# Attention ahead of a mixture of experts: rows of maxima made behind their diagonals, and a pair's first weighted values made in the next pair

## The chip, the cores and the metric

The kernel runs on one core of one Trainium2 chip. The metric is the device time in microseconds: the median of three runs was 2087.34 us (2084.76 to 2088.24). The core's engines are TensorE (PE, its weight loads PEld), VectorE (DVE), ScalarE (ACT), GpSimd (POOL) and SyncE (SP, which here starts transfers).

## The reference

Three stages follow one another. The inputs are q, k, v of shape (4, 8, 576, 64), that is 4 batches of 8 heads; the experts' weights w1 (8, 512, 1024) and w2 (8, 1024, 512); and the weights of a gated unit.

```
attn = softmax(mask(q @ k.T / sqrt(64)))          # mask by blocks of 64: block_i >= block_j
x    = attn @ v                                   # to (2304, 512)
P    = exp(x @ w_gate - max);  8 times: divide by row sums, by column sums, times N / E
out  = sum over e of P[:, e] * (relu(x @ w1[e]) @ w2[e])
y    = (silu(out @ w_gate2) * (out @ w_val2)) @ w_out2
```

The change touches the attention, and the preparation of the first two half-experts' weights that runs beside it.

## The kernel before, in words

The attention works on two heads at once, a pair; there are 16 pairs p, 4 for each batch. Scores are masked in blocks of 64 rows, so a pair has 9 block rows c of growing length. They are worked off in 8 ticks u (TICKS): u = 0 holds block rows 0 and 1, u = 1 holds 2 and 3, u = 2 to 5 hold one each (320 to 512 columns), and u = 6 and 7 hold the two halves of block row 8, 288 columns each. A tick has three thirds (three `yield`s in `attention`):

- first third: the events listed for this tick (`at`), then the scores s_u of pair p on PE, and at u = 6 the first group of weighted values, x_0 (`values(p, 0)`), and its evacuation xf (`take`);
- second third: the transposes t of the tick four earlier, one or two pending items of the split into halves (`work`), the normalising of the tick two earlier (`normalise`, GpSimd's e), the copy a of the transposes by ACT, and the maxima of this tick's scores on DVE (negm, bias);
- last third: at u = 4 the second group x_1 of the pair before and all pending items, and the exponentials e of the tick before on ACT.

Each engine works off its own list in the order in which this generator issues it. Between thirds, `w0.step()` does a step of the weights' preparation of half-experts 0 and 1 (`wowed`, 68 of 129 for each third, 29 steps each half-expert's matrix), and from the first batch's end on `fill` issues the first logits (abc_lg) and matmuls of the first experts on PE (rate 47 of 96).

Scores go to fp16 halves after the fourth pair (from there `st` tiles hold scaled halves; pairs 0 to 3 use fp32 q and k directly). The scale of a pair comes from a maximum over all partitions, which is made in three parts: `across_begin` writes a diagonal d on DVE (L103), `across_mid` multiplies it with ones on PE into a row (qk_a, v_a or w_a, L110), and `across_end` reduces the row on DVE (qk_r, w_r; L116). The row lies in a bank of the scores' pool.

PSUM's banks: three for scores and rows (`ps_s`), one for transposes (`ps_t`), one (`ps_x`) for s_7, x_0, the last transpose t_r and x_1 in turn, and three for the fill. ACT frees the bank of `ps_x` with xf.

`take` scales x_0 or x_1 into xf and appends items to `pend`: three for the first pair of a half, six for the second, which write the halves of the operands xs for the Strassen sums (hi on GpSimd or ACT, lo on GpSimd or DVE). At a batch's end all of them are worked off and `ready` lets `fill` go on with that batch's logits.

Of the kernel before, what the change touches and what calls it, by code (L numbers as in the profile page):

```python
# [9 lines left out]
F32 = mybir.dt.float32  # L10
# [20 lines left out]
def attention_moe_glu_kernel(  # L31
# [22 lines left out]
    B, NPAIR, P, S = qT.shape  # L54
    D = 64
    DM = v.shape[2]
    E, _, FF = w1.shape
# [292 lines left out]
    def expert_items(u):  # L350
# [8 lines left out]
        for i, W in enumerate((W1, W2)):  # L359
            g = {"b": [[None, None], [None, None]]}  # L360
# [34 lines left out]

            tasks = [(0, lambda k=k, mx=mx: mx(k), 1) for k in range(3)]
            tasks += [(0, lambda mx=mx, begin=begin: (mx(3), begin()), 1)]
            tasks += [(0, None, 1), (lambda force, g=g: across_made(g["r"])(force), end, 1)]
            if i == 1 and u < 2:

                def plain_sp(r, c, g=g, sp=sp):
# [403 lines left out]
    def attention(actx):  # L805
# [230 lines left out]
        def values(p, grp):  # L1036
            g = st[p]
            c0, c1 = (0, 4) if grp == 0 else (4, NC)
            a = g["a0"] if grp == 0 else g["a1"]
            nj = (c1 + 1) // 2  # L1040
            n = (c1 - c0) * CB
            x = ps_x.tile([P, 512], F32, tag="x", name=f"x_{p}_{grp}")[:, :n]
            for j in range(nj):
                f = max(c0, 2 * j)
                for h in range(2):
                    nc.tensor.matmul(
                        x[h * D : (h + 1) * D, (f - c0) * CB : n],
                        vt[p][:, j, h * D : (h + 1) * D],
                        a[:, j, f - c0 : c1 - c0, h * CB : (h + 1) * CB],
                        start=j == 0,  # L1050
                        stop=j == nj - 1,
                    )
            return x
# [62 lines left out]

        events = {}

        def at(tick, f, *a):
            events.setdefault(tick, []).append(lambda: f(*a))  # L1120

        for p in range(1, npairs):
            r = p * NTK
            if p < DIRECT:
                if p > 1:
                    at(r - NTK, load_direct, p)
                at(r - 2, lambda p: vt.update({p: load_v(*where(p), "v", 2)}), p)
                continue
            for i in range(2):
                if p > 1:  # L1130
                    at(r - 14 + 1 * i, load_qk, p, i)
                at(r - 11 + 2 * i, max_qk, p, i)
                at(r - 6 + 2 * i, hi_qk, p, i)
                at(r - 5 + 1 * i, lo_qk, p, i)
            at(r - 8, lambda p: across_mid(st[p]["m"]), p)
            at(r - 7, scale_qk, p)
            at(r - 2, lambda p: vt.update({p: load_v(*where(p), "v", 2)}), p)
        for b in range(B):
            r = (b - 1) * NPAIR * NTK
            for i in range(NPAIR):  # L1140
                if b:
                    at(r + i * NTK, scan_load, b, i)
                at(r + i * NTK + 3 if b else 1 + i, scan_max, b, i)
            r = r + NPAIR * NTK - 2 if b else NPAIR
            at(r, scale_v_begin, b)
            at(r + 1, lambda b: across_mid(vmx[b]), b)
            at(r + 2, scale_v_end, b)

        load_direct(0)
        load_direct(1)  # L1150
# [9 lines left out]
        for tk in range(tot + NTK):  # L1160
            p, u = divmod(tk, NTK)
            calm[0] = 0 < u < 5
            for f in events.pop(tk, ()):
                f()
            if on(tk):
                scores(p, u)
            if u == 6 and p < npairs:
                take(p, 0, values(p, 0))
            yield
            out1 = None  # L1170
            if on(tk - 4):
                out1 = transposes(*divmod(tk - 4, NTK))
            work(2 if len(pend) > 6 else 1)
            if on(tk - 2):
                normalise(*divmod(tk - 2, NTK))
            if out1:
                out1()
            if on(tk):
                maxima(p, u)
            yield  # L1180

            if p and u == 4:
                work(len(pend))
                take(p - 1, 1, values(p - 1, 1))
                st.pop(p - 1)
                vt.pop(p - 1)
                if p % NPAIR == 0:
                    work(len(pend))
                    ready[0] = p // NPAIR * S // 2
            if p and u == 3:  # L1190
                rest(p - 1)()
            if on(tk - 1):
                exps(*divmod(tk - 1, NTK))
            yield


# [64 lines left out]
    with tc.manual_schedule():  # L1261
# [67 lines left out]
        with ExitStack() as actx:  # L1329
            yp = actx.enter_context(tc.tile_pool(name="yp", bufs=1))  # L1330
            for _ in attention(actx):
                wowed += 68
                while wowed >= 3 * 43:
                    w0.step()
                    wowed -= 3 * 43
                if ready[0]:
                    owed += rate
                    while owed >= 3 * NTK * NPAIR:
                        next(fill, None)
                        owed -= 3 * NTK * NPAIR  # L1340
            for _ in fill:
                pass
# [411 lines left out]
```

## Time and profile before

| what | value |
| --- | --- |
| median of three runs | 2087.34 us (2084.76 to 2088.24) |
| profiled execution, span from first to last instruction | 2083.4 us |
| attention within it | 0 to 384 us |
| PE, DVE, ACT, POOL busy | 1949.0, 1620.1, 1379.9, 612.8 us |
| mean granted clock of TensorE | 0.983 |

The profiled execution is one run; no other time of it is given than its span, which lacks what lies ahead of the first and behind the last instruction. A timeline's row has the start, the duration from the first to the last of the grouped instructions, the engine, the line, the operation, its output and inputs, the shapes and the count, and in brackets the idle time before it with what ended that. A window's row has the busy time and the number of instructions of each engine, then the granted clock as a share of full speed.

### The profile page before, as it was taken

What the parts mean: (1) busy time and instruction counts of PE and PEld (TensorE: products, weight loads), DVE (VectorE), ACT (ScalarE), POOL (GpSimd) and SP (SyncE); (2) the same over time, 40 slices, a digit from 0 to 9 for tenths busy, and PEclk for the clock granted to TensorE, in tenths of its full rate; (3) what the DMA queues carried; (4) which work ended last, traced back from release to release, by engine and by line L of the source; (5) the groups of instructions that cost most, each with busy time, mean ns of one, the idle gap of its engine ahead of it and who ended that gap; (6) DMA issues with size and microseconds to landing.
All of it is one profiled execution on the core that took longest, in us unless ns stands there. A gap on an engine that the chain in (4) does not pass through costs nothing.

```text
span 2083.4 us, 47251 instructions
## 1 busy us (share of the span) xinstructions
PE 1949.0 (94%) x18378; PEld 1672.9 (80%) x18378; DVE 1620.1 (78%) x3455; ACT 1379.9 (66%) x2940; POOL 612.8 (29%) x873
## 2 busy tenths in 40 slices
PE   6789899799999999999999999999999988999998
PEld 3457676698888888888888888888888877988887
DVE  7887765668787887978878788888887877666666
ACT  5665766348777777878777777777776566544442
POOL 4534444102333333333332333333332123000000
PEclk9889999999999999999999999999999999999999
DMA  5433331306687866878668786777877100301112
GB/s 155 112 96 105 84 105 49 122 22 122 120 172 155 172 136 125 178 150 171 132 132 179 149 178 134 153 157 144 180 148 168 37 11 1 87 21 37 47 42 52
DMA packets 168721, 236.41 MB, mean 113 GB/s; under 512 B 16432, under 2 KB 85680, under 8 KB 168496
## 3 DMA queue, kind: packets, MB, share of 16 engines
q0 software_dynamic: 66560, 107.37, 30.8%
q1 hardware_dynamic: 101936, 126.01, 19.9%
q8 instruction: 144, 2.36, 0.5%
q14 instruction: 81, 0.66, 0.1%
HBM read 90.98 MB, written 24.38 MB: 55 GB/s over the span
## 4 chain that ended last, share of the span: by engine, by line
PE 55%; DVE 15%; ACT 5%; DMA 3%; issue 3%; SPq 0%; POOL 0%; ACTq 0%; DVEq 0%
PE abc_m_b L537 11%; PE m_o_b L645 11%; PE m_o_ac L645 8%; PE abc_m_c L537 5%; PE abc_m_a L537 3%; PE abc_v_b L537 3%; PE abc_g_b L537 3%; PE m_go_b L645 3%; PE m_go_ac L645 2%; DVE m_t L704 2%; DVE m_h L193 2%; DMA wr<-in_w_dram 2%; PE abc_v_c L537 1%; DVE w L182 1%; PE abc_g_c L537 1%
## 5 line engine op out<-in xcount | busy, mean ns | idle before, releaser
L537 PEld LDWEIGHTS <-w 128*128 128x128 f16 x6720 | 609.8, 98 | 110.9 <-issue 45.7
L645 PEld LDWEIGHTS <-m_h 128*128 128x128 f16 x5292 | 514.0, 98 | 69.0 <-issue 10.5
L537 PE MATMUL abc_m_b<-xs,w 128*128 128x256 f16 (+1 forms) x3840 | 476.6, 264 | 31.9 <-DVE m_t L559 29.4
L1443 POOL DMA_DIRECT2D acc<-ev x351 | 305.4, 895 | 581.3 <-ACT ev L1447 367.4
L645 PE MATMUL m_o_b<-w,m_h 128*128 128x256 f16 x3024 | 403.5, 273 | 7.9 <-ACT ev L1447 7.7
L645 PE MATMUL m_o_ac<-w,m_h 128*128 128x256 f16 x2268 | 309.4, 273 | 0.4 <-ACT ev L1447 0.4
L537 PE MATMUL abc_m_c<-xs,w 128*128 128x256 f16 (+1 forms) x1920 | 230.7, 263 | 2.2 <-DVE m_h L758 1.6
L1447 ACT ACTIVATE ev<-m_o_b,pe 128x256 f32<-128x256 f32 x351 | 161.7, 476 | 64.0 <-PE m_o_b L645 52.8
L1447 ACT ACTIVATE ev<-m_o_ac,pe 128x256 f32<-128x256 f32 (+1 forms) x234 | 135.7, 580 | 47.8 <-PE m_o_ac L645 46.4
L178 ACT ACTIVATE w<-wr,ws 128x512 f16<-128x512 f32 x210 | 150.5, 723 | 12.7 <-DVE ws L163 10.3
L182 DVE SCALAR_TENSOR_TENSOR w<-wr,ws,w 128x512 f16<-128x512 f32 x210 | 155.5, 747 | 1.4 <-ACT w L178 1.4
L1431 POOL DMA_DIRECT2D acc<-ev_s x65 | 73.6, 1132 | 259.1 <-ACT ev_s L1427 259.1
L683 ACT CAST m_h<-m_t 128x512 f16<-128x512 f32 (+1 forms) x210 | 121.8, 580 | 41.2 <-DVE m_t L704 40.3
L676 ACT ACTIVATE m_h<-m_t 128x512 f16<-128x512 f32 (+1 forms) x210 | 121.8, 582 | 35.8 <-DVE m_t L574 24.9
L193 DVE TENSOR_TENSOR m_h<-m_t,m_h 128x512 f16<-128x512 f32 (+1 forms) x210 | 133.1, 635 | 8.7 <-ACT m_h L683 8.4
L680 DVE SCALAR_TENSOR_TENSOR m_h<-m_t,m_h 128x512 f16<-128x512 f32 (+1 forms) x210 | 132.2, 635 | 5.8 <-ACT m_h L676 5.6
L537 PEld LDWEIGHTS <-gg_w 128*128 128x128 f16 x1260 | 113.5, 98 | 22.2 <-issue 10.7
L996 POOL TENSOR_SCALAR e<-e,r 128x64 f32<-128x64 f32 (+2 forms) x144 | 78.1, 548 | 166.8 <-DVE r L991 111.9
L645 PEld LDWEIGHTS <-g_h 128*128 128x128 f16 x1134 | 111.0, 99 | 18.9 <-issue 5.4
L537 PEld LDWEIGHTS <-gv_w 128*128 128x128 f16 x1260 | 113.6, 98 | 13.2 <-issue 1.7
L537 PE MATMUL abc_m_a<-xs,w 128*128 128x256 f16 (+1 forms) x960 | 117.5, 262 | 0.0
L375 DVE TENSOR_REDUCE wmx<-wr 128x1 f32<-128x512 f32 x128 | 85.7, 679 | 15.0 <-DMA wr<-in_w_dram 14.9
(298 smaller groups left out, 3364.0 us busy)
## 6 DMA issues: line engine op xcount, KB each, us to landing
acc<-ev POOLq DMA_DIRECT2D x351, 256.0 KB, 4.3
wr<-in_w_dram SPq DMA_DIRECT2D x128, 256.0 KB, 4.8
acc<-ev_s POOLq DMA_DIRECT2D x52, 256.0 KB, 4.3
st<-hl SPq DMA_DIRECT2D x48, 144.0 KB, 3.6
raw_g<-in_w_gate_dram SPq DMA_DIRECT2D x12, 512.0 KB, 5.5
raw_v<-in_w_val_dram SPq DMA_DIRECT2D x12, 512.0 KB, 4.5
raw_o<-in_w_out_dram SPq DMA_DIRECT2D x12, 512.0 KB, 5.0
scr_g<-gg SPq DMA_DIRECT2D x21, 256.0 KB, 2.9
```

The source lines that it names most:

```text
L178: nc.scalar.activation(hi, src, AF.Copy, scale=s)
L182: nc.vector.scalar_tensor_tensor(lo, src, s, hi, op0=ALU.mult, op1=ALU.subtract)
L193: nc.vector.tensor_sub(lo, src, hi)
L375: nc.vector.tensor_reduce(g["mx"][:, k : k + 1], g["b"][k // 2][k % 2], axis=AX.XY, op=ALU.max, apply_absolute_value=True)
L537: nc.tensor.matmul(ps[:, f], W[o][:, sh, k, f * P : (f + 1) * P], xs[:, o, mh, k, c0 : c0 + n], start=x not in begun, stop=True, skip_grou ...
L645: nc.tensor.matmul(ps, h[o][:, sh, k, ii * P : (ii + 1) * P], W[o][:, mh, k], start=o in (X11, X12) and k == 0 and j == 0, stop=True, skip ...
L676: nc.scalar.activation(hi, src, AF.Relu)
L680: nc.vector.scalar_tensor_tensor(lo, src, 0.0, hi, op0=ALU.max, op1=ALU.subtract)
L683: nc.scalar.copy(hi, src)
L996: nc.gpsimd.tensor_scalar(et[c][:, :n], et[c][:, :n], g["r"][:, c : c + 1], 1.0, op0=ALU.mult, op1=ALU.mult)
L1443: nc.gpsimd.dma_start(acc[:, x], e, accum_op=ALU.add)
L1447: nc.scalar.activation(e[:, cols], ps, AF.Copy, scale=p)
```

## The change

Three edits, all in the order of work; no arithmetic changes.

1. *x_0 later.* Before, x_0 of pair p was made at u = 6 of that pair in the bank of `ps_x`. Now it is made at u = 2 of pair p + 1, behind the scores s_2, in the transposes' bank. The last pair keeps the old place.
2. *Rows of maxima later.* Events have a phase: 0 at the tick's head as before, 1 behind the maxima, 2 at the tick's end behind the exponentials. The row qk_a goes to phase 2 of its tick, and its reduce with what follows (`scale_qk`) to phase 1 of the next tick. The row of v goes to phase 2, and its reduce one tick later (`at(r + 3)`), from the second batch on.
3. *Steps of the weights' lists.* For half-experts 0 and 1 three empty steps are added round the row, which splits "made and end" into two steps (29 steps become 35), and the pace goes from 68 to 80 of 129.

```diff
+            if u < 2:
+                tasks += [(0, None, 1)] * 2
+                tasks += [(lambda force, g=g: across_made(g["r"])(force), None, 1), (0, None, 1), (0, end, 1)]
+            else:
+                tasks += [(0, None, 1), (lambda force, g=g: across_made(g["r"])(force), end, 1)]
...
+            if grp == 0 and p < npairs - 1:
+                x = ps_t.tile([P, 4, P], F32, tag="t", name=f"x_{p}_{grp}").rearrange("p a b -> p (a b)")[:, :n]
...
-            at(r - 8, lambda p: across_mid(st[p]["m"]), p)
-            at(r - 7, scale_qk, p)
+            at(r - 8, lambda p: across_mid(st[p]["m"]), p, phase=2)
+            at(r - 7, scale_qk, p, phase=1)
...
-            at(r + 1, lambda b: across_mid(vmx[b]), b)
-            at(r + 2, scale_v_end, b)
+            at(r + 1, lambda b: across_mid(vmx[b]), b, phase=2 if b else 0)
+            at(r + 3 if b else r + 2, scale_v_end, b)
...
-            if u == 6 and p < npairs:
-                take(p, 0, values(p, 0))
+            if p == npairs - 1 and u == 6:
+                take(p, 0, values(p, 0))
+            elif 0 < p < npairs and u == 2:
+                take(p - 1, 0, values(p - 1, 0))
...
             if on(tk):
                 maxima(p, u)
+            happen(tk, 1)
...
             if on(tk - 1):
                 exps(*divmod(tk - 1, NTK))
+            happen(tk, 2)
...
-                wowed += 68
+                wowed += 80
```

On PE, where pair 3 follows pair 2, these rows stood in the order of before (s_6 and s_7 of pair 2, s_0 of pair 3; the names carry the tick).

```order
L931 MATMUL s_6_936<-k_528,q_527 64x288 x2
L1046 MATMUL x_0_939<-a_3_874,v_3_679 64x256 x2
L1046 MATMUL x_0_939<-a_3_874,v_3_679 64x128 x2
L1028 MATMUL t_2_947<-ident,e_132 128x128 x3
L110 MATMUL v_a<-v_d,ones 128x128
L931 MATMUL s_7_966<-k_528,q_527 64x288 x2
L1028 MATMUL t_3_969<-ident,e_134 128x128 x3
L110 MATMUL qk_a<-qk_d,ones 128x256
```

At the same place of the changed kernel there stand:

```order
L935 MATMUL s_6_936<-k_519,q_518 64x288 x2
L1032 MATMUL t_2_940<-ident,e_132 128x128 x3
L935 MATMUL s_7_956<-k_519,q_518 64x288 x2
L1032 MATMUL t_3_959<-ident,e_134 128x128 x3
L110 MATMUL v_a<-v_d,ones 128x128
```

x_0 is gone from between s_6 and t_2, and qk_a has left the place ahead of s_0; it now follows t_4. On ACT, where pair 10 follows pair 9, before (m_h and abc_m are the fill's, a the copies of the transposes t, e the exponentials of the scores s):

```order
L971 ACTIVATE e_135,sum_2806<-s_4_2962,bias_2805,sc_2484 128x448
L1061 ACTIVATE xf_9_0_3053<-x_0_3048,vs_2423 128x256
L1029 COPY a_9_3062<-t_2_3063 128x3x128
L971 ACTIVATE e_137,sum_2806<-s_5_3009,bias_2805,sc_2484 128x512
L754 ACTIVATE m_1_h_3082<-abc_m_1_b 128x512
L190 CAST xs<-xf_9_0_3053 128x128
```

and in the changed kernel, from the same exponential on:

```order
L975 ACTIVATE e_135,sum_2792<-s_4_2961,bias_2791,sc_2506 128x448
L1033 COPY a_9_3055<-t_2_3056 128x3x128
L975 ACTIVATE e_137,sum_2792<-s_5_3009,bias_2791,sc_2506 128x512
L758 ACTIVATE m_1_h_3074<-abc_m_1_b 128x512
L1033 COPY a_9_3055<-t_3_3086 128x3x128
L558 COPY abc_m_1_a<-abc_m_1_b 128x512
```

xf no longer stands between the exponential of s_4 and the copy of t_2. On POOL, at the second batch's end, before (e is the normalising, xs are the operands' halves, L1088 the sums of two xf, of which xf_6_1 and xf_7_1 belong to x_1):

```order
L996 TENSOR_SCALAR e_131<-e_131,r_2438 128x256
L1079 TENSOR_TENSOR xs<-xf_7_0_2334,xs 128x128
L996 TENSOR_SCALAR e_132<-e_132,r_2438 128x320
L1088 TENSOR_TENSOR xf_6_1_2264<-xf_6_1_2264,xf_7_1_2653 128x5x32
L1088 TENSOR_TENSOR xf_7_1_2653<-xf_7_1_2653,xf_6_1_2264 128x5x32
```

and in the changed kernel:

```order
L1000 TENSOR_SCALAR e_132<-e_132,r_2411 128x320
L188 TENSOR_SCALAR xs<-xf_6_0_2129 128x128
L188 TENSOR_SCALAR xs<-xf_7_0_2538 128x128
L1086 TENSOR_TENSOR xs<-xf_6_0_2129,xs 128x128
L1086 TENSOR_TENSOR xs<-xf_7_0_2538,xs 128x128
L1095 TENSOR_TENSOR xf_6_1_2264<-xf_6_1_2264,xf_7_1_2653 128x5x32
```

Two halves and two remainders of x_0 have come to stand between the last normalising and the first sum of x_1.

## Rows read from the trace of the kernel before

**Rows 1.** the first part of the page: busy us, share of the span, instructions.

```profile
PE 1949.0 (94%) x18378; PEld 1672.9 (80%) x18378; DVE 1620.1 (78%) x3455; ACT 1379.9 (66%) x2940; POOL 612.8 (29%) x873
```

**Rows 2.** windows, attention by stage: PE, PEld, DVE, ACT, POOL busy, PEclk, DMA, GB/s.

```profile
37.40:96.90 59.50, 45.72 (x294) 22.86 (x292) 52.98 (x175) 38.89 (x112) 34.73 (x73) 0.86 0.42 121
96.90:150.40 53.50, 41.66 (x362) 28.31 (x360) 44.65 (x127) 36.91 (x92) 21.18 (x43) 0.87 0.36 97
150.40:384.00 233.60, 216.30 (x2014) 158.33 (x2011) 154.95 (x504) 146.05 (x390) 99.60 (x225) 0.98 0.32 90
```

**Rows 3.** windows, three short stretches and all behind the attention, columns as before.

```profile
157.00:165.00 8.00, 5.60 (x57) 4.45 (x56) 6.17 (x22) 4.84 (x13) 3.59 (x8) 1.00 0.03 9
...
228.90:232.30 3.40, 3.40 (x24) 2.54 (x20) 2.45 (x12) 1.64 (x4) 0.94 (x3) 0.51 0.02 5
317.70:324.50 6.80, 6.08 (x35) 3.85 (x35) 4.24 (x20) 2.71 (x8) 1.14 (x2) 0.50 0.00 0
384.00:2083.40 1699.40, 1622.86 (x15599) 1452.23 (x15596) 1343.57 (x2571) 1142.16 (x2301) 445.71 (x491) 0.99 0.55 116
```

**Rows 4.** waits of PE, 97 to 384 us: total us, times, longest.

```profile
PE s L942 <- ACT xf L1061: 4.6, 3, 2.2
PE w_a L110 <- DVE w_d L103: 4.4, 1, 4.4
...
PE qk_a L110 <- DVE r L990: 3.5, 2, 1.8
PE t L1028 <- ACT a L1029: 3.4, 3, 1.1
PE qk_a L110 <- DVE qk_d L103: 2.5, 1, 2.5
```

**Rows 5.** timeline of PE, joint of pairs 9 and 10: start, duration, [idle before].

```profile
224.71 0.44 PE L942 MATMUL s<-st,st 128*64 128x288 f16 x4 [1.56 <-ACT xf L1061]
...
228.12 0.70 PE L110 MATMUL qk_a<-qk_d,ones 128*128 128x256 f32 x2 [1.77 <-DVE r L990]
```

**Rows 6.** timeline of ACT, the same joint.

```profile
224.20 0.46 ACT L1061 ACTIVATE xf<-x,vs 128x256 f32<-128x256 f32 x1
...
225.59 0.21 ACT L971 ACTIVATION_READ_ACCUMULATOR e<-s,bias,sc 128x1 f32 x1
```

**Rows 7.** timeline of DVE, the start.

```profile
12.43 0.82 DVE L843 TENSOR_REDUCE vmx<-v_first 128x1 f32<-128x640 f32 x1
...
15.92 0.69 DVE L375 TENSOR_REDUCE wmx<-wr 128x1 f32<-128x512 f32 x1 [1.08 <-DMA wr<-in_w_dram]
...
16.80 0.54 DVE L954 TENSOR_REDUCE negm<-s 128x1 f32<-128x384 f32 x1
```

**Rows 8.** timelines of PE and DVE, pair 3, second and third tick.

```profile
64.16 0.76 PE L931 MATMUL s<-k,q 64*64 64x320 f32 x4
...
63.81 0.29 DVE L116 TENSOR_REDUCE w_r<-w_a 128x1 f32<-128x128 f32 x1 [0.68 <-PE w_a L110]
...
65.87 0.32 DVE L963 TENSOR_SCALAR bias<-negm 128x2 f32<-128x2 f32 x1
```

**Rows 9.** timelines of PE and DVE, pair 9, second and third tick.

```profile
207.58 0.42 DVE L116 TENSOR_REDUCE qk_r<-qk_a 128x2 f32<-128x256 f32 x1
...
211.04 0.32 DVE L963 TENSOR_SCALAR bias<-negm,sc 128x2 f32<-128x2 f32 x1
...
210.47 0.46 PE L942 MATMUL s<-st,st 128*64 128x320 f16 x4
```

**Rows 10.** timelines of POOL and PE, batch's start and end.

```profile
104.85 0.30 POOL L188 TENSOR_SCALAR xs<-xf 128x128 f16<-128x128 f32 x1
...
106.16 0.73 POOL L188 TENSOR_SCALAR xs<-s 128x128 f16<-128x128 f32 x1
...
197.33 0.43 POOL L1079 TENSOR_TENSOR xs<-xf,xs 128x128 f16<-128x128 f32 x1
...
200.87 0.46 PE L1207 MATMUL abc_lg<-wg,xs 128*128 128x16 f16 x12 [0.46 <-DVE xs L193]
```

More of the change, by code (lines that the diff above doesn't have):

```diff
@@ L397, in expert_items @@
             tasks += [(0, lambda mx=mx, begin=begin: (mx(3), begin()), 1)]
-            tasks += [(0, None, 1), (lambda force, g=g: across_made(g["r"])(force), end, 1)]
+            if u < 2:
[3 more added lines that the diff above has]
+                tasks += [(0, None, 1), (lambda force, g=g: across_made(g["r"])(force), end, 1)]
             if i == 1 and u < 2:
@@ L1041, in values @@
             n = (c1 - c0) * CB
-            x = ps_x.tile([P, 512], F32, tag="x", name=f"x_{p}_{grp}")[:, :n]
+            if grp == 0 and p < npairs - 1:
+                x = ps_t.tile([P, 4, P], F32, tag="t", name=f"x_{p}_{grp}").rearrange("p a b -> p (a b)")[:, :n]
+            else:
+                x = ps_x.tile([P, 512], F32, tag="x", name=f"x_{p}_{grp}")[:, :n]
             for j in range(nj):
@@ L1117, in attention, with at, happen @@
         events = {}
-        def at(tick, f, *a):
-            events.setdefault(tick, []).append(lambda: f(*a))
+        def at(tick, f, *a, phase=0):
+            events.setdefault((tick, phase), []).append(lambda: f(*a))
+        def happen(tick, phase):
+            for f in events.pop((tick, phase), ()):
+                f()
         for p in range(1, npairs):
@@ L1162, in attention @@
             calm[0] = 0 < u < 5
-            for f in events.pop(tk, ()):
-                f()
+            happen(tk, 0)
             if on(tk):
                 scores(p, u)
-            if u == 6 and p < npairs:
+            if p == npairs - 1 and u == 6:
                 take(p, 0, values(p, 0))
+            elif 0 < p < npairs and u == 2:
+                take(p - 1, 0, values(p - 1, 0))
             yield
```

## The prediction

> **What bounds the kernel now.** I began with the first part of the page: TensorE is busy for 94% of the span, no other engine for more than 78% [rows 1]. The edits touch only the attention, which ends at 384 us; behind it PE works 1622.86 of 1699.40 us at a granted clock of 0.99 [rows 3], and nothing there moves, so that part keeps its length. Next I split the attention by stage. From 37.4 to 96.9 us DVE is busy 52.98 of 59.50 us: VectorE is the limit, and a TensorE wait that goes there buys little. From 96.9 to 150.4 us DVE has 44.65 and PE 41.66 of 53.50 us: no engine is full, the chain between them is the limit. From 150.4 us PE has 216.30 of 233.60 us: PE is the limit, each wait of PE is time, and the matmuls of the first half-experts fill the rest [rows 2].
>
> Then the list of what PE waits for from 97 to 384 us, sorted by what ended the wait: scores held by ACT's xf 4.6 us in 3 places, a row of weights' maxima 4.4 us in one, rows of q and k held by DVE 3.5 us in 2 and 2.5 us in 1, transposes held by ACT's copies 3.4 us in 3 [rows 4]. All of these lie where one pair of heads follows another; I call this place the joint. Last I read one joint, pair 9 to 10. The scores s_7 start 1.56 us late because the bank that they share with x_0 is freed by ACT's xf, and the row qk_a starts 1.77 us late, behind DVE [rows 5]. In between ACT works off xf (0.46 us) and the exponentials of s_5, whose sum is read by 225.80 us [rows 6].
>
> **The change part by part.** The sum is made against the span of the profiled execution, 2083.4 us. The median of the three runs shown is 2087.34, so 3.9 us lie around the span; I add them at the end.
>
> *x_0 leaves the joint.* Its matmuls and ACT's xf are the same work in another place; only the waits differ. At the joint of pair 9, s_7 finds its bank free, as x_1 left it long before, and qk_a now stands behind the transposes t_4. Without the first wait PE stands at 224.79 where it stood at 226.35 (228.12 less 1.77 less 1.56). ACT is next late: without the 0.46 us of xf it has read s_5 at 225.34 (225.80 less 0.46). So a wait of 0.55 us takes the place of 1.56 + 1.77 = 3.33 us: -2.8 us. The joint near 318 us has the rest of these rows, 4.6 - 2.2 - 1.56 = 0.84 us and the other 1.77 us [rows 4], in all 2.61 us, less 0.55: -2.1 us. Bounds for each: nothing, and the whole wait.
>
> *The clock behind these two waits.* Behind them the granted clock is 0.51 for 3.40 us and 0.50 for 6.80 us, with PE busy 3.40 and 6.08 us [rows 3]; that is the lower level, 1.2 GHz. The same work at 2.4 GHz takes half: up to 1.7 + 3.0 = 4.7 us. A joint whose transposes waited 1.1 us kept 1.00 over its 8 us [rows 3, 4]. The rows therefore speak for the fall going with the wait, but two places are few, and a new wait elsewhere may bring a fall of its own: I take half, -2.4 us (0 to -4.7).
>
> *Three joints where transposes wait for ACT's copies* (3.4 us [rows 4]): xf, 0.46 us [rows 6], no longer stands ahead of those copies: 3 x 0.5 = -1.5 us (0 to -3.4).
>
> *The first two joints with fill work.* Their waits are s_7's 2.2 us for xf, a row's 2.5 us and the weights' row's 4.4 us, both behind DVE [rows 4]. DVE has the same work to do afterwards and only 53.50 - 44.65 = 8.85 us idle. I take the first alone: -2.2 us (0 to -8.85).
>
> *The direct phase.* The reduce of a weights row, which waited 0.68 us for its PE row [rows 8], now has a free step between the two: -0.7 us. The other end is the next part's.
>
> *The row's bank.* The row's reduce, qk_r (0.42 us), moves on DVE behind the maxima of s_1. Its bank goes to s_2, so s_2 gains a wait, and all of PE's queue stands behind it, transposes and fill too. At pair 9 the bias of s_1 ends at 211.36; with qk_r behind it the bank is free at 211.78, where s_2 started at 210.47: 1.31 us [rows 9]. The maxima of s_1 come some 0.5 us sooner when ACT has no xf ahead of its exponentials, so I take 0.8, here and at pair 13, which has the same pattern: +1.6 us (0 to 2.6). At pair 3 the same sum gives 65.87 + 0.32 + 0.42 - 64.16 = 2.45 us [rows 8], but there DVE is the limit and qk_r is none of new work: nothing (0 to +2.5). The Trainium skill, "PSUM — Partial Sum Buffer", section "Engine vs sequencer instructions", says that the queues of ScalarE, VectorE and GpSimd are strictly first in, first out. By that rule qk_r can't pass the maxima of s_1 and every pair pays its full lateness, which is rival B below, 2096.1 us; no row of before shows qk_r in the new place, so the chance of B is not raised for it.
>
> *The end of a batch.* x_0's later items, four on GpSimd (two halves of 0.30, two remainders of 0.43 us: 1.46 us [rows 10]), were done by then; now they stand ahead of x_1's sum, on whose operands the logits wait in PE's queue (0.46 us already). PE gets about 1.3 us each at the second and third batch end, and 0.4 at the first, where DVE is the limit: +3.0 us. The same 128x128 half took 0.73 us elsewhere [rows 10], so the lump can reach 1.46 x 0.73/0.30 = 3.5 us; below, POOL's idle time may hide it: 0 to +7.5 us in all. The Trainium skill, "GPSIMD Engine Reference", section "8. Key points", says that GpSimd shares its SBUF interfaces with VectorE and contends with DVE instructions that read two SBUF inputs. The two durations above agree with it; with all four items stretched the two batch ends would cost 7 us, and the sum would be near no change.
>
> *The start.* The first wmx, which waits for its weights until 15.92 us, now stands ahead of two vmx reduces of 0.82 us, with a second wmx (0.69) behind them and only then s_3's maxima, which were made at 16.80 [rows 7]. They come at 15.92 + 2 x 0.69 + 2 x 0.82 + 0.3 = 19.2, 2.5 us later. Since x_0 and its xf leave this stretch (some 1.3 us of PE and ACT there), I take +1.2 us (0 to +2.5). The empty steps in the weights' lists come with the faster pace (29 steps at 68, 35 at 80): nothing.
>
> Sum: 1.2 - 0.7 - 2.2 - 2.8 - 2.1 - 2.4 - 1.5 + 1.6 + 3.0 = -5.9 us; span 2077.5, time 2081.4 us.
>
> **The rivals.** *A: PE is full at every joint.* All waits that name xf, DVE's row or w_d go, 4.6 + 4.4 + 3.5 + 2.5 = 15.0 us [rows 4], and the clock's 4.7; against it stand the losses of 5.8: -13.9 us, 2073.4 us. For it: PE is the limit from 150 us on. Against it: DVE's 44.65 of 53.50 us before that.
>
> *B: s_2's wait decides, slower.* ACT's queue keeps s_1 where it is, so the joints give nothing, and every pair waits for qk_r. Pair by pair as above, pairs 3 and 4 lose 2.5 and 1.2, the later twelve 5.1 together (only pairs 9 and 13 above 1 us): +8.8 us, 2096.1 us. It decides once the mean wait of the 14 pairs is over (5.9 + 1.6) / 14 = 0.54 us. For it: at pair 3, s_1 already waited for qk_r's engine, and s_2 starts before the bias of s_1 at pair 9. Against it: the exponentials move forward with xf gone.
>
> *C: the wait only moves.* x_0 needs the transposes' bank, so t_7 waits for xf and x_0 for t_5's copy, and what the joint gave goes in the third tick: 2087 us. For it: one bank, and PE full there. Against it: the third tick has no transposes of its own between x_0 and t_7, so xf has the whole tick.
>
> **How the numbers follow.** Forecast 0.50, A 0.17, B 0.19, C 0.14. A measurement of this kernel tells about 0.2%, 4.2 us, from no change. Of the forecast's chance two thirds lie beyond it: faster 0.33 + 0.17 = 0.50; same 0.17 + 0.14 = 0.31; slower 0.19. The likeliest case by its own terms is 2077 to 2087. The range goes to 2071 below, past A, and to 2094 above, which leaves out half of B and a part of A.
>
> **What would show it.** Right: from 222 to 235 us s_7 without a wait for xf and qk_a without one for DVE; fewer stretches at the lower clock from 150 to 384 us; the logits at each batch end waiting longer on xs; s_2 waiting for qk_r at pairs 9 and 13, under 1 us. Wrong: s_2 waiting over half a microsecond in most pairs (B), t_7 or x_0 waiting for ACT in the third tick (C), a new stretch at the lower clock where there was none, or a stretch from 37 to 150 us that changes by more than 3 us, where I hold DVE to be the limit.

## The result

The changed kernel takes 2099.90 us (median of 5 runs, 2090.71 to 2100.88), before 2084.76 us in the same comparison (5 runs): a ratio of 1.0058 with a 95% interval of 1.0044 to 1.0072. By the ratio it is slower by some 12 us (the medians are 15.1 us apart), where 5.9 us of gain were forecast; the time lies outside the stated range. The span of the profiled execution grew from 2083.4 to 2099.1 us. That execution is the longest of the five, so what follows by place shows somewhat more loss than the ratio.

The first part of the page after:

```profile
PE 1962.0 (93%) x18378; PEld 1680.9 (80%) x18378; DVE 1619.3 (77%) x3455; ACT 1380.9 (66%) x2940; POOL 611.2 (29%) x873
```

PE is busy for 13 us more [rows 1], though it does the same 18378 matmuls: more of them ran at the lower clock, and the mean granted clock is 0.976 where it was 0.983. The windows of the same stages, each cut where s_5 of the same pair starts (pairs 1, 4 and 6), and the rest (columns as in [rows 2]):

```profile
41.80:107.00 65.20, 48.74 (x291) 24.68 (x291) 51.98 (x172) 39.31 (x112) 32.12 (x71) 0.79 0.40 118
107.00:158.60 51.60, 41.68 (x364) 28.39 (x362) 44.39 (x126) 36.98 (x93) 19.14 (x41) 0.90 0.33 92
158.60:399.70 241.10, 218.89 (x2002) 158.87 (x1999) 156.21 (x506) 146.42 (x389) 101.53 (x229) 0.96 0.30 87
399.70:2099.10 1699.40, 1628.28 (x15610) 1457.11 (x15608) 1342.10 (x2571) 1142.85 (x2302) 445.96 (x491) 0.99 0.55 116
```

The stage bound by VectorE took 5.7 us more, the middle one 1.9 us less, the stage bound by PE 7.5 us more; the rest behind the attention took the same 1699.40 us [rows 2, 3]. With 4.4 us more ahead of the first window that is the whole 15.7 us. So all of it lies in the attention, as said. The larger part, 10.1 us, lies ahead of s_5 of pair 4. In the first window the granted clock fell from 0.86 to 0.79, and VectorE, busy for 51.98 of 65.20 us where it was 52.98 of 59.50, stood idle for 13.2 us in place of 6.5: it did not fill that stage any more. PE's waits from 97 to 400 us after:

```profile
PE t L1032 <- ACT a L1033: 10.5, 6, 2.4
PE s L946 <- ACT e L975: 7.8, 10, 2.3
PE abc_lg L1221 <- DVE xs L193: 5.7, 6, 2.1
PE s L946 <- DVE qk_r L116: 2.4, 5, 0.5
...
PE s L946 <- DVE v_r L116: 0.9, 2, 0.4
...
PE qk_a L110 <- DVE r L994: 0.6, 2, 0.3
```

and two more rows of before, from 97 to 384 us as in [rows 4]:

```profile
PE s L942 <- ACT e L971: 3.7, 4, 1.3
...
PE abc_lg L1207 <- DVE xs L193: 2.4, 6, 0.5
```

Against these and [rows 4]: no score waits for xf any more, and the rows qk_a wait 0.6 us in place of 3.5 + 2.5. But transposes wait 10.5 us for ACT's copies in place of 3.4, the logits 5.7 us in place of 2.4, the scores 7.8 us for the exponentials in place of 3.7 (2.5 of the 7.8 lie ahead of pair 4's s_5 at 107 us, which is before the start of the other window), and two waits are new here, for qk_r and v_r.

A pair-by-pair comparison says where. The start of s_5 of each pair was read in both timelines; this table gives how much longer each stretch from one s_5 to the next is than before, in us (the first, to pair 4, from the span's start; all are single profiled executions; e1 to e10 are told in the next section). The joints near 159, 228, 250 and 318 us of before lie in the stretches 6-7, 9-10, 10-11 and 13-14, the batch ends at 200 and 291 us in 8-9 and 12-13.

| kernel | to 4 | 4-6 | 6-7 | 7-8 | 8-9 | 9-10 | 10-11 | 11-12 | 12-13 | 13-14 | 14-15 | sum |
| --- | --- | --- | --- | --- | --- | --- | --- | --- | --- | --- | --- | --- |
| changed | 10.10 | -1.93 | 1.80 | 0.71 | 4.09 | -2.39 | 1.69 | 0.71 | 4.06 | -3.52 | 0.36 | 15.68 |
| x_0 alone (e1) | 0.08 | 1.95 | 3.85 | 0.01 | 3.28 | 0.05 | 1.29 | 0.00 | 3.25 | -1.03 | 0.44 | 13.17 |
| rows and lists (e2) | 4.04 | -2.10 | 0.00 | 0.67 | 0.83 | -2.69 | 0.01 | 0.67 | 0.81 | -3.82 | 0.00 | -1.58 |
| lists alone (e3) | 3.97 | -2.64 | 0.00 | 0.00 | 0.00 | 0.01 | 1.63 | 0.00 | -0.01 | -1.13 | 0.00 | 1.83 |
| batch ends old (e4) | 8.33 | -1.89 | 1.68 | 0.66 | 0.85 | -2.40 | 1.69 | 0.66 | 0.81 | -3.53 | 0.36 | 7.22 |
| reduce early (e5) | 5.85 | -2.70 | 1.25 | 0.85 | 3.28 | -2.60 | 2.24 | 0.84 | 3.24 | -3.74 | 0.41 | 8.92 |
| two rows (e6) | -0.49 | -0.10 | -0.01 | 0.00 | -0.01 | -2.17 | 0.01 | 0.00 | 0.00 | -3.32 | 0.00 | -6.09 |
| x_0 alone, old bank (e7) | 2.20 | 0.84 | 2.81 | -0.01 | 3.30 | 0.05 | 1.26 | 0.00 | 3.29 | -1.05 | 0.42 | 13.12 |
| x_0 in two pairs (e8) | 0.65 | 0.00 | 0.59 | 0.00 | 0.00 | -0.19 | 1.96 | 0.00 | 0.00 | -1.28 | 0.00 | 1.72 |
| items early (e9) | 7.51 | -1.72 | 1.78 | 0.71 | 3.34 | -2.41 | 1.63 | 0.72 | 1.55 | -3.56 | 0.36 | 9.91 |
| direct pairs old (e10) | 5.78 | -1.94 | 1.62 | 0.65 | 0.85 | -2.40 | 1.64 | 0.66 | 0.81 | -3.54 | 0.36 | 4.49 |

From pair 7 on a stretch with the same order of work repeats from kernel to kernel within a few tenths, but where a stretch at the lower clock comes, stays away or is longer: e3 has before's order there and shows 1.63 us at 10-11, with a fall of the clock at 254 us, and e1 and e3 win 1.0 and 1.1 at 13-14, where before stood at the lower clock for 6.80 us [rows 3]. The stretches before pair 7 move by up to 2.7 us between kernels that are alike there (the changed kernel, e4 and the kernel e9 issue the same work to pair 2 and reach its s_5 at +4.00, +3.25 and +1.30; e6 and e8 have before's order to pair 3 and reach its s_5 at +0.14 and +2.23).

The changed kernel and x_0 alone have like sums, but not in the same places: x_0 alone loses nothing by pair 4 and 5.8 us from there to pair 7, the changed kernel 10.1 us by pair 4 and nothing from there to pair 7.

**The batch ends.** The rows of POOL at the second batch's end behind the last normalising, the next row of DVE, and the logits on PE behind it:

```profile
210.64 0.69 POOL L188 TENSOR_SCALAR xs<-xf 128x128 f16<-128x128 f32 x2
211.30 0.81 POOL L1086 TENSOR_TENSOR xs<-xf,xs 128x128 f16<-128x128 f32 x2
212.07 0.52 POOL L1095 TENSOR_TENSOR xf<-xf,xf 128x160 f32<-128x160 f32 x1
```

```profile
212.62 0.33 DVE L1095 TENSOR_TENSOR xf<-xf 128x160 f32<-128x160 f32 x1 [1.71 <-POOL xf L1095]
```

```profile
213.23 0.46 PE L1221 MATMUL abc_lg<-wg,xs 128*128 128x16 f16 x12 [2.14 <-DVE xs L193]
```

x_0's two halves and two remainders (0.69 and 0.81 us; I call these four items the lump) stand between the normalising and the first sum of x_1, and DVE waits 1.71 us for that sum. The logits wait 2.14 us where it was 0.46 [rows 10]: 1.68 us. That was forecast as 1.3. What had no price of its own in the forecast follows it: the granted clock falls to the lower level. Windows of the four such stretches of the stage bound by PE:

```profile
167.20:170.60 3.40, 3.22 (x12) 2.25 (x13) 2.68 (x9) 1.54 (x3) 2.07 (x5) 0.50 0.03 7
215.00:218.40 3.40, 3.40 (x19) 2.12 (x17) 3.00 (x13) 2.12 (x6) 1.92 (x5) 0.50 0.65 186
262.80:266.20 3.40, 2.99 (x17) 2.02 (x17) 2.68 (x7) 2.18 (x6) 1.89 (x5) 0.50 0.00 0
310.60:314.00 3.40, 3.40 (x18) 2.10 (x17) 3.05 (x14) 1.98 (x5) 1.97 (x4) 0.50 0.11 30
```

From 215.0 us PE works 3.40 us at 0.50, work that takes half at the upper level: 1.7 us more. Together 3.4 us, and the same again at 310 us. The falls of before at the joints near 228 and 318 us [rows 3] are gone, but four others are there.

**The joint of pairs 6 and 7.** PE after (the transposes t_4, the scores s_1), and ACT:

```profile
167.24 1.08 PE L1032 MATMUL t<-ident,e 128*128 128x128 f32 x4 [2.29 <-ACT a L1033]
...
170.86 0.57 PE L946 MATMUL s<-st,st 128*64 128x192 f16 x8 [0.41 <-ACT e L975]
```

```profile
165.35 1.15 ACT L758 ACTIVATE m_h<-m_t 128x512 f16<-128x512 f32 x2 [2.18 <-DVE m_t L578]
166.41 0.31 ACT L190 CAST xs<-xf 128x160 f16<-128x160 f32 x1
166.62 0.47 ACT L1033 COPY a<-t 128x384 f32<-128x384 f32 x1
```

and the same of before:

```profile
159.00 0.63 PE L1028 MATMUL t<-ident,e 128*128 128x128 f32 x4 [1.14 <-ACT a L1029]
...
161.54 0.57 PE L942 MATMUL s<-st,st 128*64 128x192 f16 x8 [1.26 <-ACT e L971]
```

```profile
157.34 1.15 ACT L754 ACTIVATE m_h<-m_t 128x512 f16<-128x512 f32 x2 [1.28 <-DVE m_t L574]
158.40 0.46 ACT L1029 COPY a<-t 128x384 f32<-128x384 f32 x1
```

In both the copy a that t_4 waits for stands on ACT behind the fill's m_h, which waits for DVE's m_t (1.28 us before, 2.18 after). No xf stands between them. After, a cast of operands' halves (0.31 us) has come in between. Taking x_0 (0.82 us) and qk_a (0.60) out of PE's list ahead of t_4 let PE arrive earlier, and wait 2.29 us instead of 1.14; the next wait, for the exponentials, fell from 1.26 to 0.41. The sum of the two waits is 2.70 against 2.40. In e2, which moves the row and not x_0, it stays 2.40 (1.58 + 0.82); in e8, which moves x_0 and not the row, it is 2.72 (1.46 + 1.26), and there too such a cast (0.31 us at 158.77) stands ahead of the copy. So x_0's move adds 0.3 us of waiting here and saves none; that the cast is the cause fits, but no run takes it away alone. The rest of the stretch's 1.80 us goes with the fall of the clock: PE works 3.22 us at 0.50 from 167.2 us, some 1.6 us more than at the upper level.

**Pair 3.** There the late reduce meets a row of the weights' maxima. PE after, and a window behind it:

```profile
68.30 0.77 PE L110 MATMUL w_a<-w_d,ones 128*128 128x128 f32 x2 [1.41 <-DVE qk_r L116]
```

```profile
68.00:76.00 8.00, 6.37 (x29) 3.15 (x29) 2.63 (x15) 3.80 (x13) 1.56 (x5) 0.57 0.00 0
```

The row w_a took the bank of qk_a and waited 1.41 us for qk_r; before, w_a at that place did not wait. PE then ran at a mean clock of 0.57 over 8 us.

**The start.** DVE's maxima of s_3, then PE's row of v after and before:

```profile
19.06 0.54 DVE L958 TENSOR_REDUCE negm<-s 128x1 f32<-128x384 f32 x1
```

```profile
21.76 0.77 PE L110 MATMUL v_a<-v_d,ones 128*128 128x128 f32 x2 [8.55 <-DVE v_d L103]
```

```profile
19.51 0.76 PE L110 MATMUL v_a<-v_d,ones 128*128 128x128 f32 x2 [6.21 <-DVE r L990]
```

s_3's maxima came at 19.06, forecast as 19.2; v_a was 2.25 us later, and s_5 of pair 1 came 4.4 us later (41.80 against 37.40). In e1 it came 1.34 us earlier, near the 1.3 us that x_0's leaving was to give back, but stretches here move that much by themselves; in the changed kernel nothing of it shows.

### The profile page after: what moved, and what is told of

Read it like the earlier page. It is cut to its first block, busy times and chain, and to the rows that moved or that the text cites. A ratio compares the mean times of both kernels' runs of the same rounds, so it can differ in the third digit from the quotient of the medians.

```text
span 2099.1 us, 47214 instructions
## 1 busy us (share of the span) xinstructions
PE 1962.0 (93%) x18378; PEld 1680.9 (80%) x18378; DVE 1619.3 (77%) x3455; ACT 1380.9 (66%) x2940; POOL 611.2 (29%) x873
## 4 chain that ended last, share of the span: by engine, by line
PE 54%; DVE 15%; ACT 4%; DMA 3%; issue 3%; SPq 0%; POOL 0%; ACTq 0%; DVEq 0%
PE abc_m_b L541 11%; PE m_o_b L649 11%; PE m_o_ac L649 8%; PE abc_m_c L541 5%; PE abc_m_a L541 3%; PE abc_v_b L541 3%; PE abc_g_b L541 3%; PE m_go_b L649 3%; PE m_go_ac L649 2%; DMA wr<-in_w_dram 2%; DVE m_t L708 2%; DVE m_h L193 2%; PE abc_v_c L541 1%; PE abc_g_c L541 1%; DVE w L182 1%
## 5 line engine op out<-in xcount | busy, mean ns | idle before, releaser
L649 PEld LDWEIGHTS <-m_h 128*128 128x128 f16 x5292 | 514.0, 98 | 68.5 <-issue 10.1
```

The costliest lines, as they stand in the source:

```text
L649: nc.tensor.matmul(ps, h[o][:, sh, k, ii * P : (ii + 1) * P], W[o][:, mh, k], start=o in (X11, X12) and k == 0 and j == 0, stop=True, skip ...
```

## The experiments

Each was timed in turn with the kernel before on the same chip, and a ratio is to before's runs beside it; before's median lay between 2084.8 and 2087.1 us in these comparisons, so differences between medians of two comparisons are good to 2 us; differences between ratios don't contain the movement of before.

**e1, x_0 alone.** Theory D (displaced work), made from the traces of before and after, says that x_0's move is the loss.

```diff
+            if grp == 0 and p < npairs - 1:
+                x = ps_t.tile([P, 4, P], F32, tag="t", name=f"x_{p}_{grp}").rearrange("p a b -> p (a b)")[:, :n]
...
+            if p == npairs - 1 and u == 6:
                 take(p, 0, values(p, 0))
+            elif 0 < p < npairs and u == 2:
+                take(p - 1, 0, values(p - 1, 0))
```

> Only the move of x_0 (edit 1); rows and weights' lists as before. Theory D (displaced work): where PE waits at a joint for the chain of VectorE and ScalarE behind the fill (m_t, m_h, copy of t_3), taking x_0's 0.82 us away only lengthens the wait, and x_0 costs its 0.82 us in the next pair's third tick, where PE is full; the two batch ends at 200 and 290 us lose 1.7 us each at the logits and some 1.8 us each to the lower clock behind it; the joints at 228 and 318 us lose their waits for xf and give back 2 to 3 us each. Sum +3 to +6 us, 2088 to 2091. Rival S (start): the changed kernel's loss lies in the weights' lists and the rows, and x_0 alone gains: -3 to -6 us, 2079 to 2082.

2097.67 us against 2085.73, ratio 1.0054 (1.0041 to 1.0067): nearly the whole loss, twice what D expected; rival S, which expected a gain, falls. The 2 to 3 us that D expected back at the joints near 228 and 318 us are not there. The joint of pairs 9 and 10 in e1, on PE (t_3, then qk_a):

```profile
233.80 0.52 PE L1028 MATMUL t<-ident,e 128*128 128x128 f32 x3 [1.77 <-ACT a L1029]
...
236.75 0.89 PE L110 MATMUL qk_a<-qk_d,ones 128*128 128x256 f32 x2 [1.77 <-DVE r L990]
```

and what stands ahead of xf on ACT before, and ahead of the copy for t_3 on ACT in e1:

```profile
222.44 1.15 ACT L754 ACTIVATE m_h<-m_t 128x512 f16<-128x512 f32 x2 [2.09 <-DVE m_t L574]
```

```profile
231.44 1.15 ACT L754 ACTIVATE m_h<-m_t 128x512 f16<-128x512 f32 x2 [1.91 <-DVE m_t L574]
```

The wait of s_7 for xf, 1.56 us [rows 5], is gone, and 1.77 us of waiting for ACT's copy stands one step later; qk_a waits the same 1.77 us for DVE. In both kernels ACT is late because the fill's m_h waits about 2 us for DVE's m_t, and what stands behind it in ACT's list, xf before and the copy in e1, is late with it. Moving x_0 gave that joint 0.05 us of loss, not 2.8 us of gain; the 1.03 us won at 13-14 come in e3 too (1.13), with x_0 in its old place. This is the step of the prediction that failed.

**e2, the rows and the lists without x_0.**

```diff
+            at(r - 8, lambda p: across_mid(st[p]["m"]), p, phase=2)
+            at(r - 7, scale_qk, p, phase=1)
...
+                wowed += 80
```

> Edits 2 and 3 without 1: rows late and the weights' lists changed, x_0 at its old place at tick 6 in the old bank. Theory D: the start's later v_a and pairs 3 and 4 stay slow, the five waits of s_2 for qk_r (0.45 us each) stay, the logits wait 0.46 us as before: +4 to +9 us, 2089 to 2094. Rival B (the row's bank decides): s_2's waits make nearly all of the loss: +12 to +15 us, 2097 to 2100. Rival X (x_0 makes nearly all of it): within 3 us of before.

2085.15 us, ratio 0.9998 (0.9989 to 1.0008): no change. Rival X, that x_0 makes nearly all of the loss, holds; D's +4 to +9 and B's +12 do not. The same joint (s_7, qk_a, s_2):

```profile
227.62 0.44 PE L946 MATMUL s<-st,st 128*64 128x288 f16 x4 [1.04 <-ACT xf L1065]
...
231.03 0.70 PE L110 MATMUL qk_a<-qk_d,ones 128*128 128x256 f32 x2 [0.28 <-DVE r L994]
...
235.01 0.46 PE L946 MATMUL s<-st,st 128*64 128x320 f16 x4 [0.47 <-DVE qk_r L116]
```

With x_0 at its old place the row's wait fell from 1.77 to 0.28 us, and s_7's from 1.56 to 1.04. The late rows gave the joints their 2.69 and 3.82 us, with s_2's new wait of 0.47 us within them; 1.1 of the 3.82 come with the lists alone too (e3).

**e3, the lists alone.**

```diff
+            if u < 2:
+                tasks += [(0, None, 1)] * 2
...
+                wowed += 80
```

> Only edit 3: the weights' lists with their empty steps, at the pace of 80. Theory D: wmx stands ahead of the maxima of v in VectorE's order, v_a comes some 2.3 us later, and that stays to the end: +2 to +5 us, 2087 to 2090. Rival: VectorE is idle for 37 us of the first 97, so the later v_a is made up for by pair 4: within 1 us of before.

2089.49 us, ratio 1.0016 (1.0007 to 1.0024): +3.8 us, as D expected. In its profile 4.0 us are lost by pair 4 and 2.6 of them won back by pair 6, where the last row of the weights waits 1.75 us for DVE's diagonal in place of 4.4 [rows 4]:

```profile
135.11 0.80 PE L110 MATMUL w_a<-w_d,ones 128*128 128x128 f32 x2 [1.75 <-DVE w_d L103]
```

Behind that a fall of the clock near 255 us adds 1.6. Part of the 3.8 us is therefore not placed by the profile, which shows 1.8 by s_5 of the last pair. The rival, that the loss is made up for by pair 4, falls (VectorE's idle time in the first 97 us of before, with 76.9 us busy, is 20 us and not the 37 that it named). The lists without the late rows cost; the late rows on top of them bring 2085.15 - 2089.49 = -4.3 us. Late rows for all pairs with the old lists were not tried.

**e4, x_0 of the batches' last pairs at the old place.**

```diff
-            if grp == 0 and p < npairs - 1:
+            if grp == 0 and p % NPAIR < NPAIR - 1:
...
+            if p < npairs and p % NPAIR == NPAIR - 1 and u == 6:
                 take(p, 0, values(p, 0))
...
+            elif 0 < p < npairs and p % NPAIR and u == 2:
```

> The changed kernel, with x_0 of each batch's last pair (pairs 3, 7, 11) at its old place, tick 6 in the old bank, so that its items on GpSimd are done before x_1's sums. Theory D: the logits wait 0.46 us again instead of 2.14 at two batch ends, and the lower clock that follows for 3.8 us each goes: -5 to -8 us against the changed kernel, 2092 to 2095. Rival: the operands are late by their own chain (ACT's xf of x_1, then sums), so the logits still wait over 1.5 us: within 2 us of the changed kernel, 2098 to 2101.

2090.62 us, 9.3 us under the changed kernel's 2099.90 by the medians and 7.5 by the ratios; ratio to before 1.0022 (1.0010 to 1.0033). The logits at the second batch's end:

```profile
209.65 0.46 PE L1221 MATMUL abc_lg<-wg,xs 128*128 128x16 f16 x12 [0.46 <-DVE xs L193]
```

The stretches 8-9 and 12-13 fall from 4.09 and 4.06 to 0.85 and 0.81 us: 3.2 us each, the wait's 1.68 and the clock's 1.7. D's mechanism holds, and the rival, that the operands are late by their own chain, falls. The two stretches make 6.5 us; 1.8 more lie before pair 4, where stretches move that much by themselves.

**e5, the reduce early.** The row stays late, qk_r goes back ahead of s_1's maxima.

```diff
-            at(r - 7, scale_qk, p, phase=1)
+            at(r - 7, scale_qk, p)
```

> The changed kernel with the reduce qk_r back at the head of its tick (before s_1's maxima); the row itself stays late. Theory D: only the waits of s_2 for qk_r go (0.45 to 0.49 us, five from 97 us on): -1 to -3 us against the changed kernel. Rival B (the row's bank): those waits hold up the fill behind them too, -8 us against it.

2092.77 us, ratio 1.0039 (1.0024 to 1.0055), 7.1 us under the changed kernel by the medians and 4.0 by the ratios; the two intervals overlap. Neither expectation holds as written. By place: from pair 4 on it is 2.5 us shorter, as D said (the waits of s_2 at pairs 9 and 13, 0.8 us each with what goes with them). The rest, 4.3 us, lies before pair 4, where w_a no longer waits for qk_r (68.30 above); stretches there move by up to 2.7 us by themselves. As far as that goes, rival B's mechanism, the bank, did bite there, with w_a as the one who waits.

**e6, two rows late and nothing else.**

```diff
+            late = p in (11, 15)
+            at(r - 8, lambda p: across_mid(st[p]["m"]), p, phase=2 if late else 0)
+            at(r - 7, scale_qk, p, phase=1 if late else 0)
```

> Before, with only two rows late: those of pairs 11 and 15, which stand at the joints near 228 and 318 us; their reduces behind s_1's maxima; nothing else changed. Theory D: the two joints give 2.7 and 3.8 us as with all rows late, and none of the other pairs loses: -5 to -7 us, 2079 to 2081. Rival: the gain there came with the weights' lists or the fill's later phase, and alone the rows give nothing: within 2 us of before.

2080.03 us against 2086.49, ratio 0.9974 (0.9961 to 0.9986): faster than both kernels. D holds, and the rival, that the rows alone give nothing, falls. PE at the joint of pairs 9 and 10 (qk_a, then s_2):

```profile
224.10 0.44 PE L942 MATMUL s<-st,st 128*64 128x288 f16 x4 [1.56 <-ACT xf L1061]
...
227.50 0.70 PE L110 MATMUL qk_a<-qk_d,ones 128*128 128x256 f32 x2 [0.27 <-DVE r L990]
...
231.48 0.46 PE L942 MATMUL s<-st,st 128*64 128x320 f16 x4 [0.46 <-DVE qk_r L116]
```

s_7 still waits its 1.56 us for xf, qk_a waits 0.27, s_2 0.46; the stretch is 2.17 us shorter, the other 3.32, of which some 1.1 is what e1 and e3 win there as well. No stretch of it from 150 to 370 us has the lower clock.

**e7, x_0 at the new place in the old bank.**

```diff
-            if u == 6 and p < npairs:
+            if p == npairs - 1 and u == 6:
+                take(p, 0, values(p, 0))
+            elif 0 < p < npairs and u == 2:
+                take(p - 1, 0, values(p - 1, 0))
```

> Before, with x_0 in the next pair's third tick as in the change, but still in its old bank (that of s_7 and x_1). Theory D: the place costs, not the bank: +10 to +13 us, as with x_0 in the transposes' bank. Rival C (the bank): the transposes' bank makes t_7 or x_0 wait, so without it the loss is under 4 us.

2097.51 us, ratio 1.0061 (1.0044 to 1.0077), as with the transposes' bank (e1: 1.0054), and as D expected. The place costs, the bank does not; rival C of the prediction falls.

**e8, x_0 late in pairs 6 and 10 alone.**

```diff
+            if grp == 0 and p in (6, 10):
+                x = ps_t.tile([P, 4, P], F32, tag="t", name=f"x_{p}_{grp}").rearrange("p a b -> p (a b)")[:, :n]
...
+            if u == 6 and p < npairs and p not in (6, 10):
                 take(p, 0, values(p, 0))
+            elif u == 2 and p - 1 in (6, 10):
+                take(p - 1, 0, values(p - 1, 0))
```

> Before, with x_0 moved for pairs 6 and 10 alone (the joints near 159 and 250 us, where the transposes wait 1.14 us for ACT's copy); no batch's end is touched. Theory D: the wait at the joint grows by about x_0's 0.82 us, and its work is done again where PE is full: +1.5 to +4 us, 2087 to 2090. Rival (the prediction's own term): xf gone from ACT's queue makes those copies earlier: -1 us.

2087.81 us, ratio 1.0008 (0.9996 to 1.0020): not told from no change. PE at the joint of pairs 6 and 7 (t_4, s_1):

```profile
159.60 0.63 PE L1028 MATMUL t<-ident,e 128*128 128x128 f32 x4 [1.46 <-ACT a L1029]
...
162.14 0.57 PE L942 MATMUL s<-st,st 128*64 128x192 f16 x8 [1.26 <-ACT e L971]
```

The wait grew from 1.14 to 1.46, by 0.32 and not by the 0.82 that D said, and the second stayed 1.26. The prediction's -0.5 a joint is not there either. The two stretches are at +0.59 and +1.96 us, the second with a fall of the clock at 253 us, which e3 had there with before's order in place. The changed kernel and the kernels e4, e5, e9 and e10, which have x_0 and qk_a both gone from these joints, show 1.25 to 2.24 us at both of them each time; e2 and e6 show nothing.

**e9, x_0's items earlier.** The changed kernel, two items a tick ahead of each batch's end.

```diff
-            work(2 if len(pend) > 6 else 1)
+            work(2 if len(pend) > 6 or (p and p % NPAIR == 0 and 2 <= u <= 4) else 1)
```

> The changed kernel with two pending items instead of one in ticks 2 to 4 of each batch's first pair, so that x_0's items (pairs 3, 7, 11) are worked off by tick 4 and don't stand in one lump ahead of x_1's sums. Theory D (the lump, and the lower clock behind the logits' wait): the logits wait 0.5 us instead of 2.14, -5 to -8 us against the changed kernel, 2092 to 2095. Rival (x_0's operands are simply late, wherever their items stand): the logits still wait 1.5 us or more, within 2 us of the changed kernel.

2094.49 us, ratio 1.0032 (1.0021 to 1.0043): 5.4 us under the changed kernel. The logits at the second and third batch end:

```profile
210.09 0.46 PE L1221 MATMUL abc_lg<-wg,xs 128*128 128x16 f16 x12 [1.39 <-DVE xs L193]
```

```profile
303.54 0.46 PE L1221 MATMUL abc_lg<-wg,xs 128*128 128x16 f16 x12 [0.55 <-DVE xs L193]
```

At the third end the wait is 0.55 us and no lower clock follows: the stretch is at 1.55 us, 2.5 under the changed kernel. At the second it is 1.39 us, the clock falls at 212 us, and the stretch gains only 0.75. Another 2.6 us of the profile's gain lie before pair 4, within what stretches there move by themselves. Half a success: the logits' wait goes with the lump, and spreading it is not always enough.

**e10, x_0 of the first four pairs at the old place as well.**

```diff
-            if grp == 0 and p < npairs - 1:
+            if grp == 0 and p >= NPAIR and p % NPAIR < NPAIR - 1:
...
+            if p < npairs and (p < NPAIR or p % NPAIR == NPAIR - 1) and u == 6:
                 take(p, 0, values(p, 0))
...
+            elif NPAIR < p < npairs and p % NPAIR and u == 2:
```

> As the kernel e4 (batch ends at the old place), and x_0 of pairs 0 to 3 at the old place too, so that x_0 is late in pairs 4 to 6, 8 to 10 and 12 to 14 alone; rows and weights' lists as changed. Theory D: the 4 us that e4 has above e2 by pair 4 go: -3 to -5 us against e4, 2086 to 2088, and what is left above e2 is the three joints at 1.7 us or less each. Rival: the direct pairs are held by VectorE whatever x_0 does: within 1.5 us of e4.

2090.01 us, ratio 1.0012 (1.0003 to 1.0021), 0.6 us under e4 by the medians, which is the rival's side, and 2.1 by the ratios, which is neither's; the intervals of the two ratios overlap. By the profiles it reaches pair 4 at +5.78 us where e4 has +8.33 and e2 +4.04, and s_5 of the last pair comes 2.7 us sooner than in e4. So what x_0 costs in the direct pairs stays open between 0.6 and 2.7 us.

## Why the prediction was wrong

**x_0 leaves the joint (-2.8 and -2.1): wrong.** This is the step that failed. It took the releaser that the timeline names, xf, for the cause, and x_0's move for a gain; alone the move cost 11.9 us (e1), and without it the other two edits came out at no change (e2). xf was late because ACT itself was late behind the fill's m_h and DVE's m_t (222.44 above); with xf gone, PE met the same lateness at the next transposes, 1.77 us in e1 and 1.41 in the changed kernel where 0.55 was forecast. The joints did gain 2.39 and 3.52 us, but by the late rows (e2, e6), which the prediction had counted as a help to x_0's move. That the number came out near is luck: it is another edit's gain.

**Three joints (-1.5): wrong in sign.** +1.80, +1.69 and +0.36: the copies were not held by xf, and PE came earlier into the same wait (167.24 above). At the first two a fall of the clock makes most of it.

**The clock (-2.4): half right.** The two falls went as forecast. That a new wait might bring a fall of its own was said, and half of the gain was left out of the sum for that and for the small number of places; what came were four falls, two at the batch ends and two at the joints, each of 1.5 to 1.7 us by PE's busy time in the windows above.

**The batch's end (+3.0): mechanism right, size wrong.** The lump lasted as the shorter rows said, 0.69 us for two halves against 0.30 for one [rows 10]. The contention with VectorE of which the Trainium skill speaks ("GPSIMD Engine Reference", "8. Key points") could not show in these rows, for DVE stood idle beside most of the lump (212.62 above). Nor do the two durations of before tell it: the half of 0.30 us at 104.85, too, ran beside a DVE instruction with two inputs (w<-wr,ws,w, 104.83 to 105.68). In e9 the same two remainders took 1.31 us at the third end (300.57), beside DVE's hl<-qk,qk_s,hl, and 0.81 at the second (207.64), without such a one beside them: one place that fits. The forecast 1.3 us a batch end became 3.2, half of it the clock. The first end, at 109 us, cost nothing (0.45 us as before).

**The row's bank (+1.6): right where PE bounds.** The rows at pair 9: DVE's bias of s_1 and the late reduce, PE's s_2:

```profile
223.88 0.34 DVE L967 TENSOR_SCALAR bias<-negm,sc 128x2 f32<-128x2 f32 x1
224.13 0.41 DVE L116 TENSOR_REDUCE qk_r<-qk_a 128x2 f32<-128x256 f32 x1
```

```profile
...
224.59 0.46 PE L946 MATMUL s<-st,st 128*64 128x320 f16 x4 [0.49 <-DVE qk_r L116]
```

s_2 waits 0.49 us and s_1 0.22; the stretch costs 0.83 us without x_0 (e2), forecast 0.8. So the Trainium skill's rule that VectorE's queue is strictly first in, first out ("PSUM — Partial Sum Buffer", "Engine vs sequencer instructions") agrees with the trace: qk_r starts at 224.13, behind the bias of s_1. The full price of rival B needs PE to stand where it stood before, and it did not: s_1 itself came later. Two things were missed: v_r, which holds s_1 for 0.45 us at each new batch (0.7 us a stretch in e2), and pair 3, set at nothing because VectorE is the limit there: PE waited 1.41 us and lost clock, 4.0 us by the difference of the changed kernel and e5 from s_5 of pair 2 to that of pair 3 (3.59 against -0.43; e4 and e9, with the same row there, have 2.99 and 3.63).

**The first joints with fill (-2.2): not shown.** Pairs 4 to 6 gained 1.93 us, but the lists alone gave 2.64 there (e3), by the weights' row, which the sum had at nothing; and s_7's wait for xf, 2.2 us, became 2.40 us of t_3 waiting for ACT.

**The start (+1.2), the direct phase (-0.7), pair 3 (nothing): far too small.** In size this is the largest miss: 0.5 us forecast by pair 4, 10.10 measured. The chain of DVE was worked out to 0.2 us; the 1.3 us taken off for x_0 don't show in the changed kernel. Nor do the 0.7 us: pair 1's scores behind the first weights' row waited 1.11 us for the exponentials before (31.13) and wait 1.15 for w_r after (34.47). The premise, that VectorE is the limit and PE's waits buy and cost little there, did not hold (13.2 us of idle time in the first window). The lists cost 3.97 us by pair 4 alone (e3) and 4.04 with the late rows (e2), x_0 alone 0.08 (e1). The other 6 us come only with all three edits, less with the reduce early (e5, 5.85) or x_0 old in these pairs (e10, 5.78). How they divide stays open, since these are single executions of stretches that move by themselves.

**The rivals.** B gave 2096.1 us, the nearest number, by a mechanism that accounts for 1.6 us in the stage bound by PE and some 4 us in pair 3. A and C fell. The case that came true, x_0's displaced work with a lower clock behind longer single waits, stood among the prediction's conditions but not among its rivals. Last, the 3.9 us around the span compared one execution with another's median: runs after have 2100.88 us for a span of 2099.1, 1.8 us.

## What to carry to other kernels

The releaser that a profile names is the last link of a chain: before pricing its removal, follow that engine's own queue one wait further, and ask what PE meets next when it arrives earlier. Taking work out of PE's list ahead of a wait shortens nothing if the wait grows by as much; here the waits of a joint grew by 0.3 us, and a fall of the clock often came with them. Follow displaced work to every engine that it feeds: the largest losses behind pair 4, 3.2 us at each of two batch ends, came from four GpSimd items that had been done early and came to stand ahead of the logits' operands. Move only the items whose place gains: two of the rows gave 5.4 us by the ratio, all the edits together lost some 12.

## What the runs showed of the hardware

In the stage bound by PE a single wait of 2.14 to 2.29 us was followed by 3.40 us at a granted clock of 0.50, four times out of four in the changed kernel (the windows above). At the batch ends the fall, 1.7 us, doubled the price of the 1.68 us by which the wait had grown.

It is not a matter of the length alone. In e1 the same pair of waits, 1.46 us at t_4 and 1.26 us at s_1, stood at two joints; the clock was low behind the first and full behind the second:

```profile
162.00:168.80 6.80, 5.54 (x32) 3.79 (x31) 4.83 (x17) 2.33 (x6) 3.07 (x7) 0.50 0.01 4
260.00:266.80 6.80, 5.54 (x54) 4.50 (x55) 5.36 (x21) 4.25 (x13) 3.27 (x7) 1.00 0.00 0
```

In e5 a longer wait than any in the changed kernel's PE-bound stage, at the joint of pairs 6 and 7, left it at full:

```profile
162.76 0.63 PE L1032 MATMUL t<-ident,e 128*128 128x128 f32 x4 [2.83 <-ACT a L1033]
```

```profile
162.80:169.60 6.80, 5.98 (x56) 4.86 (x58) 5.35 (x21) 4.16 (x12) 3.27 (x7) 1.00 0.01 4
```

So did 1.58 and 0.82 us one after the other in e2, at two joints, and 1.41 us at transposes in e4, while 1.39 us at the logits in e9 was followed by a fall. What decides is not shown by these runs; a price for a fall is therefore a chance times 1.5 to 1.7 us.
